# RetNet scores and an MLP on one core: scalings of q and k, their transposes and the loads put into other slots of a tile

## The chip, the core and the metric

The kernel runs on one core of a Trainium2 chip. Time is device microseconds (us) of one execution. The engines are TensorE (PE in the profile; PEld is its weight load), VectorE (DVE), ScalarE (ACT), GpSimd (POOL) and SyncE (SP). Each takes its instructions in its own order and waits on semaphores for the others. DMA transfers are issued from SyncE's queue (outputs and transposes) and GpSimd's (loads), and run on 16 DMA engines.

## What is computed

```python
scores = (1 / sqrt(64)) * q @ k^T                  # q, k, v: 8 batches x 8 heads x 576 x 64
ret = scores * Dmat                                # gamma_h ** (i - j) for i >= j, else 0
x = (ret @ v) as 4608 rows x 512
h = x @ w_in                                       # 512 x 2048
out = (h * tanh(softplus(h))) @ w_out              # 2048 x 512
```

## The kernel before

**Chunks and tiles.** The rows are cut into 36 chunks of 128. Four chunks are a tile; tiles 0 to 8 go through the MLP one after the other. Chunks 0 to 7 are handled in a way of their own. A later chunk n goes through these steps:

- the loads of q and k into `qkraw` and of v into `vs` (`load_part`, L326), issued from GpSimd; `qkraw` has 5 buffers, `vs` 10. A load can be paced (`paced`, L312): it is issued only after a given activation of ScalarE.
- the scaling P(n) (`step_p`, L344): two VectorE instructions at L352 multiply q and k by powers of gamma, row by row, into `qks` (bf16, 6 buffers).
- the transpose T(n) (`step_t`, L355): from chunk 16 on a DMA transpose at L374 on SyncE's queue, from `qks` to `qkT` (6 buffers).
- the scores (`step_s`, L377, products at L386) and the mask (`step_m`, L390, VectorE at L392) for a pair of chunks.
- the states (`states`, L422; products at L432 take `qks` and `vs`, VectorE sums them up at L454 and L456).
- the outputs (`outputs`, `outputs_end`, products at L488 and L504), copied by ScalarE (L516, L561) into `xT`, which the MLP reads.

A *visit* does the outputs of a pair n, n + 1 and the states and scores of the pair after it. `outputs_end` comes in two groups, and the second must not start before the first has been written: `written` (L415) puts a no-op on SyncE's queue that waits for the first group, and TensorE's second group at L504 waits for this no-op. It is called the *marker* here (L417). In a whole visit (`visit`, L518) both groups stand in one slot, with the scores of the next pair between them. In a split one (`visit_first`, L538; `visit_second`, L550) the marker comes four slots ahead of the second group.

**The steady loop** (L1151 to L1243) runs tiles t = 2 to 7. Each has 16 slots i: tile t's first MLP product with its activation (`g1`, L581; ScalarE L587), the second product of tile t - 1 (`unit`, L742, in Strassen's manner with 7 products of half sizes; `g_sum` on VectorE at L650 forms the sums that it takes), and the attention of the next tile. `PLAN` (L1128) lists the jobs of the slots from tile 3 on: g is a `g1`, U a unit, S a `g_sum`, X the sums of `xT`, A and B the two parts of a pair of Strassen blocks in the first product. A (`pair_begin`, L817) makes four products, ScalarE copies two of them (L830, L831), and GpSimd adds them up (L832, L833). B (`pair_end`, L836) makes three more, and VectorE subtracts (L844) and adds (L846); ScalarE's activation L845 then frees the PSUM bank. By slots, A0 is in 2, B0 in 3, A1 in 11, B1 in 12.

With n the first chunk of the half (n = 4(t + 1), + 2 from slot 8 on), a half of a tile from 3 on goes like this, with slots counted from the half's start: P(n + 4) at the end of slot 4, P(n + 5) at the end of slot 5, T(n + 4) and T(n + 5) at the start of slot 7. A whole visit is in slot 6 of its half; split ones are in 2 and 6. Whole are those with n = 16, 20, 22, 26, 28 and 32: the first halves of tiles 3, 4, 6 and 7, the second halves of 4 and 5. In tile 2, P(16) and P(17) are in slots 3 and 5, P(18) and P(19) in 10 and 12; T(16) is in slot 4, T(17) in 7, T(18) in 12, T(19) in 13.

In tiles from 3 on `LOADS` (L1148) places twelve loads: the v's of chunks n + 6 and n + 7 (n of the first half) in slots 2 and 3, their q's and k's in 4 to 7, the v's of n + 8 and n + 9 in 8 and 9, their q's and k's in 11 to 14.

The output rows of tile t - 1 are sent from SyncE (`send`, L610) after unit 9 (VectorE L699, slot 10) and after unit 13 (VectorE L712, slot 15).

Of the kernel before, what the change touches and what calls it, by code (L numbers as in the profile page):

```python
# [9 lines left out]
F32 = mybir.dt.float32  # L10
BF16 = mybir.dt.bfloat16
# [5 lines left out]
def kernel(  # L17
# [19 lines left out]
    B, H, S, D = q.shape  # L37
    assert (B, H, S, D) == (8, 8, 576, 64)
    P = 128
# [5 lines left out]
    NCH = 4  # L45
    NPE = 16
# [17 lines left out]
    io = ctx.enter_context(tc.tile_pool(name="io", bufs=PF))  # L64
    tok = ctx.enter_context(tc.tile_pool(name="tok", bufs=6))
# [12 lines left out]
    live = {}  # L78
# [233 lines left out]
    def paced(ins):  # L312

        while pace:
            behind(ins, pace.pop())
        return ins
# [8 lines left out]

    def load_part(n, part):  # L326
        b, c = chunks[n]
        if n not in live:
            qkr = io.tile([P, 2, H, D], F32, name="qkraw")
            live[n] = {"qkr": qkr, "vs": tok.tile([P, H, D], BF16, name="vs", bufs=10)}  # L330
        qkr, vr = live[n]["qkr"], live[n]["vs"]
        for t, src in (((qkr[:, 0], q), (qkr[:, 1], k), (vr, v))[part],):
            live[n]["landing"] = []
            if c < 4:
                ins = nc.gpsimd.dma_start(out=t, in_=src[b, :, ds(P * c, P), :].rearrange("h p d -> p h d"))  # L335
                live[n]["landing"].append(paced(ins))
            else:
                for e in range(2):
                    ins = nc.gpsimd.dma_start(
                        out=t[ds(64 * e, 64)],  # L340
                        in_=src[b + e, :, ds(512, 64), :].rearrange("h p d -> p h d"))
                    live[n]["landing"].append(paced(ins))
# [131 lines left out]
    def run(jobs, *how):  # L474
        while jobs:
            jobs.pop()(*how)
# [145 lines left out]
    NS = 2  # L622
# [47 lines left out]
    def rest():  # L670
        while behind_visit:
            behind_visit.pop(0)()
# [96 lines left out]
    def w_in_sum_first(i):  # L769

        a, b, op_ = W7[i]
        to = {1: kept[:, 0], 5: kept[:, 1], 6: kept[:, 2]}.get(i)
        if to is None:
            to = w_in_quarter(*{2: (1, 0), 7: (0, 1)}[i])
        nc.vector.tensor_tensor(to, w_in_quarter(*a), w_in_quarter(*b), op=op_)
        w7[i, 0] = to
# [16 lines left out]
    def x_sums(t):  # L793

        if not x_room:
            x_room.append(first.tile([P, 2, H, D], BF16, name="k0", bufs=2).rearrange("p x h d -> p (x h d)"))
            x_room.append(first.tile([P, 2, NP, 64], F32, name="s0", bufs=4)
                          .rearrange("p x n d -> p (x n d)").bitcast(BF16))
            x_room.append(consts.tile([P, hK * hT], BF16, name="xsum"))
        x = lambda j, k: xts[t][:, ds(hK * j, hK), ds(hT * k, hT)]  # L800
        for m, (i, a, b, op_) in enumerate(((3, (0, 1), (1, 1), OP.subtract), (4, (1, 0), (0, 0), OP.subtract),
                                            (6, (0, 0), (0, 1), OP.add), (1, (0, 0), (1, 1), OP.add),
                                            (7, (1, 0), (1, 1), OP.add))):
            x7[i] = x_room[m // 2][:, ts(m % 2, hK * hT)].rearrange("p (c k) -> p c k", c=hK)
            nc.vector.tensor_tensor(x7[i], x(*a), x(*b), op=op_)
        x7[5], x7[2] = x(1, 1), x(0, 0)
# [152 lines left out]
    def att(n, steps):  # L959
        if n >= n_chunks:  # L960
            return
        for step in steps:
            {"P": step_p, "T": step_t}[step](n)
# [117 lines left out]
    for u in range(2, 24):  # L1081
        j, w = divmod(u, 4)
# [54 lines left out]
            pace.append(done[t])  # L1137

    def load_ahead(t, i, so_far):
        for at in (x for x in range(12) if LOADS[x] == i):  # L1140
            m, part = ((0, 2), (1, 2), (0, 0), (0, 1), (1, 0), (1, 1))[at % 6]
            n = NCH * (t + 1) + at // 6 * 2 + 6 + m
            if n < n_chunks:
                if so_far:
                    pace.append(so_far)
                load_part(n, part)

    LOADS = (2, 3, 4, 5, 6, 7, 8, 9, 11, 12, 13, 14)  # L1148
    W_IN = {4: (1, 2), 5: (6, 5), 13: (7,)}
    W_IN_FIRST = {7: 1, 8: 5, 9: 6, 10: 2, 11: 7}  # L1150
    for t in range(NS, nT - 1):  # L1151
        for i in range(nF):
            n, w = NCH * (t + 1) + i // 8 * 2, i % 8
            copies_first = i == 8 and n - 2 in WHOLE
            if w == (2 if t == NS else 0) and not copies_first:
                run(casts, act)
            if t == NS and i in W_IN_FIRST:
                w_in_sum_first(W_IN_FIRST[i])
            if t == nT - 2 and i == 15:
                rest()  # L1160
                x_sums(nT - 1)
            for m in W_IN.get(i, ()) if t == nT - 2 else ():
                w_in_sum(m)
            if (t, i) in HALVED:
                halved[0] = HALVED[t, i]
            for job in PLAN[i] if t > NS else {5: ("S5",), 9: ("S7",)}.get(i, ()):
                if job[0] == "S":
                    g_sum(t - 1, int(job[1]))
                elif job == "X":
                    x_sums(t)  # L1170
            if t == NS:
                if w == 6:
                    visit(n, ((ps_h, "hp"), (ps_h, "hp")), (act, act))
            elif n in WHOLE:
                if w == 6:
                    visit(n, ((ps_h, "hp"), (ps_h, "hp")), (act, act))
                elif w == 7:
                    run(sums)
            elif w == 2 and n < n_chunks:
                visit_first(n)  # L1180
            elif w == 6 and n < n_chunks:
                visit_second(n, act)
            if w == (3 if t > NS else 7 if n + 2 == NPE else 0) or w == 0 and n + 2 == NPE:
                run(sums)
            if w in (0, 1) and n + 2 < NPE:
                att(n + 2 + w, "P")
            if w == 1 and n + 4 == NPE:
                more_loads(n + 7)
            ahead = (2, 4) if n + 2 == NPE else (3, 5)
            if t == NS and w in ahead and n + 4 >= NPE:  # L1190
                att(n + 4 + ahead.index(w), "P")
            if t == NS and i == 11:
                behind_visit.pop(0)()
            if t == NS and i == 13:
                rest()
            if w == 0 and n + 2 == NPE:
                tick(t)
            if w == 7 and n + 4 == NPE:
                att(n + 5, "T")
            if w == (4 if n <= NPE - 2 else 7) and n + 4 >= NPE:  # L1200
                att(n + 4, "T")
            if t == NS and n + 2 >= NPE and w in PACED:
                m, part = ((0, 2), (1, 2), (0, 0), (0, 1), (1, 0), (1, 1))[PACED.index(w)]
                tick(t)
                load_part(n + 6 + m, part)
            if w == 5 and n + 4 < NPE:
                more_loads(n + w + 2)
            if w in (4, 5) and n + 2 < NPE:
                att(n - 2 + w, "T")
            if w == (5 if n + 2 == NPE else 7) and n + 2 >= NPE:  # L1210
                att(n + 5, "T")

            if t == NS:
                if i == 14:
                    for s in (2, 3):
                        send(t - 1, s)
                if w == 6:
                    unit(t - 1, BESIDE[i])
                g1(t, i)
                if i in BESIDE and w != 6:  # L1220
                    unit(t - 1, BESIDE[i])
            else:
                if i == 15:
                    rest()
                so_far = done.get(t)
                jobs = PLAN[i]
                for job in reversed(jobs) if n in WHOLE and w == 6 else jobs:
                    if job[0] == "A":
                        pair_begin(int(job[1]))
                    elif job[0] == "B":  # L1230
                        pair_end(t, int(job[1]))
                    elif job[0] == "g":
                        g1(t, int(job[1:]))
                    elif job[0] == "U":
                        unit(t - 1, int(job[1:]))
                        run(crossed)
                        if copies_first:
                            run(casts, act)
                if w in (4, 5):
                    att(n + w, "P")  # L1240
                load_ahead(t, i, so_far)
                if i == 8:
                    rest()  # L1243
# [32 lines left out]
```

## Time and profile before

| what | value |
|---|---|
| median of 3 runs | 284.32 us (284.06, 284.32, 287.03) |
| profiled execution | 283.5 us |
| its span | 281.8 us |
| mean granted TensorE clock | 0.999 |
| DMA: loads from GpSimd (q0) | 25.44 MB, 66.0% of 16 engines' span |
| DMA: outputs and transposes from SyncE (q1) | 14.69 MB, 28.8% |

A row of a timeline has the start in us from the span's start, the duration, the engine and the line, output and inputs, and how many instructions of one kind were merged; a bracket tells how long the engine had been idle before it, and what ended that. A row of waits has the sum, the times and the longest. SPq is SyncE's sequencer: the duration of a DMA there is the time for which it holds SyncE, not that of the transfer. A row of a stretch of time has each engine's busy time, then the granted clock, the DMA share and GB/s. Tile 3 begins at about 98.8 us, tile 4 at 127.2, tile 5 at 155.6, tile 6 at 184.0 and tile 7 at 212.5; a slot is about 1.8 us.

### The profile page before, as it was taken

How to read it: one execution, taken by the hardware profiler on the slowest of the kernel's cores; microseconds unless marked ns; L12 is line 12 of the kernel's file. 1: busy time of each engine (PE TensorE's matmuls, PEld its weight loads, DVE VectorE, ACT ScalarE, POOL GpSimd, SP SyncE). 2: the span in 40 equal slices, each digit the busy share in tenths (PEclk: the TensorE clock that was granted, in tenths of full speed). 3: DMA queues.
4: the chain of work that ended last, by engine and by line, in shares of the span. 5: the costliest groups of instructions: out<-in, count | busy, mean ns of one | idle time of the engine just before them, and what ended most of it. 6: DMA issues, size and time to landing. Idle time of an engine off the chain costs nothing.

```text
span 281.8 us, 9378 instructions
## 1 busy us (share of the span) xinstructions
PE 275.0 (98%) x4036; PEld 206.0 (73%) x4036; DVE 225.1 (80%) x350; ACT 165.9 (59%) x303; POOL 142.1 (50%) x177
## 2 busy tenths in 40 slices
PE   7899999999999999999999999999999999999994
PEld 3566788988866677667777776777767766888783
DVE  4864679979988978887897978787898786778783
ACT  5555566645886566665675565656566656567620
POOL 8848395877582725472558074718121002559400
PEclk9999999999999999999999999999999999999999
DMA  7999999999999989989999999999956002200333
GB/s 153 158 202 189 193 213 174 192 199 240 185 206 128 178 254 149 148 198 81 231 163 183 119 189 149 238 74 219 105 142 141 2 2 78 74 2 0 113 97 91
DMA packets 77161, 41.24 MB, mean 146 GB/s; under 512 B 60736, under 2 KB 69184, under 8 KB 77120
## 3 DMA queue, kind: packets, MB, share of 16 engines
q0 software_dynamic: 49872, 25.44, 66.0%
q1 hardware_dynamic: 26656, 14.69, 28.8%
q8 instruction: 31, 0.51, 0.8%
q10 hardware_dynamic: 592, 0.52, 0.6%
q14 instruction: 10, 0.08, 0.1%
HBM read 36.70 MB, written 9.44 MB: 164 GB/s over the span
## 4 chain that ended last, share of the span: by engine, by line
PE 93%; DVE 2%; DMA 2%; ACT 1%; issue 1%; POOLq 0%; SPq 0%; POOL 0%; ACTq 0%; DVEq 0%
PE ops L659 28%; PE hp L571 26%; PE hp L598 5%; PE hp L810 5%; PE st L659 5%; PE hp L659 4%; PE hp L576 2%; PE st L810 2%; PE sc L432 2%; DMA gT<-in_q_dram 2%; PE sc L386 2%; PE sc L810 1%; PE sc L923 1%; PE sc L366 1%; PE hp L488 1%; PE hp L504 1%
## 5 line engine op out<-in xcount | busy, mean ns | idle before, releaser
L571 PE MATMUL hp<-xT,w_in_t 128*128 128x512 bf16 x340 | 84.9, 379 | 0.1
L659 PEld LDWEIGHTS <-room 128*128 128x128 bf16 x656 | 63.3, 98 | 15.4
L587 ACT ACTIVATE gT<-hp 128x512 bf16<-128x512 f32 x93 | 55.1, 598 | 30.3 <-PE hp L571 30.2
L650 DVE TENSOR_TENSOR room<-gT 128x2048 bf16<-128x2048 bf16 x43 | 52.5, 1240 | 1.1 <-ACT gT L587 1.1
L571 PEld LDWEIGHTS <-w_in_t 128*128 128x128 bf16 x344 | 33.2, 98 | 27.2 <-issue 0.5
L832 POOL TENSOR_TENSOR k<-k 128x256 f32<-128x256 f32 x10 | 9.5, 951 | 62.2 <-ACT k L830 62.2
L659 PE MATMUL ops<-room,room 128*128 128x256 bf16 x320 | 39.9, 273 | 0.0
L352 DVE TENSOR_TENSOR qks<-qkraw,gqk 128x512 bf16<-128x512 f32 x56 | 35.1, 682 | 0.1
L659 PEld LDWEIGHTS <-gT 128*128 128x128 bf16 x288 | 27.6, 98 | 6.4 <-ACT gT L587 0.4
L659 PE MATMUL ops<-w_out_t,room 128*128 128x256 bf16 x224 | 28.7, 273 | 0.0
L335 POOL DMA_DIRECT2D vs<-in_v_dram x24 | 21.6, 902 | 12.7 <-ACT gT L587 12.7
L335 POOL DMA_DIRECT2D qkraw<-in_q_dram x24 | 21.8, 908 | 9.9 <-DMA vs<-in_v_dram 8.6
L335 POOL DMA_DIRECT2D qkraw<-in_k_dram x24 | 21.6, 899 | 9.8 <-ACT gT L587 9.6
L844 DVE TENSOR_TENSOR k<-k,hp 128x512 f32<-128x512 f32 x10 | 6.9, 686 | 17.7 <-PE hp L810 12.8
L392 DVE TENSOR_TENSOR sm<-sc,mask 128x1024 bf16<-128x1024 f32 x14 | 17.0, 1217 | 2.4 <-PE sc L386 2.3
L598 PE MATMUL hp<-xT,w_in_t 128*128 128x128 bf16 (+1 forms) x184 | 15.3, 240 | 0.0
L456 DVE TENSOR_TENSOR total<-sc,total 128x256 f32<-128x256 f32 x32 | 13.5, 422 | 0.8
L598 PEld LDWEIGHTS <-w_in_t 128*128 128x128 bf16 x184 | 13.1, 98 | 1.1 <-DVE xT L255 0.2
L516 ACT CAST xT<-hp 128x512 bf16<-128x512 f32 x18 | 9.7, 589 | 6.4 <-PE hp L504 6.3
L845 ACT ACTIVATE gT<-hp 128x512 bf16<-128x512 f32 x10 | 6.0, 597 | 11.8 <-DVE k L844 11.8
L601 ACT ACTIVATE gT<-hp 128x512 bf16<-128x512 f32 x16 | 9.6, 600 | 5.4 <-PE hp L598 5.4
L659 PE MATMUL ops<-w_out_t,gT 128*128 128x256 bf16 x96 | 12.5, 273 | 0.0
(205 smaller groups left out, 512.0 us busy)
## 6 DMA issues: line engine op xcount, KB each, us to landing
out_dram<-res SPq DMA_DIRECT2D x29, 256.0 KB, 4.6
qkraw<-in_q_dram POOLq DMA_DIRECT2D x24, 256.0 KB, 5.6
qkraw<-in_k_dram POOLq DMA_DIRECT2D x24, 256.0 KB, 5.9
vs<-in_v_dram POOLq DMA_DIRECT2D x24, 128.0 KB, 4.8
w_out_t<-in_moe_w_out_dram POOLq DMA_DIRECT2D x4, 512.0 KB, 12.0
w_in_t<-in_moe_w_in_dram POOLq DMA_DIRECT2D x6, 256.0 KB, 8.2
out_dram<-res SPq DMA_DIRECT2D x9, 128.0 KB, 2.5
qkraw<-in_q_dram POOLq DMA_DIRECT2D x8, 128.0 KB, 5.2
```

The lines of the kernel that those rows point to most:

```text
L335: ins = nc.gpsimd.dma_start(out=t, in_=src[b, :, ds(P * c, P), :].rearrange("h p d -> p h d"))
L352: nc.vector.tensor_tensor(slots[:, :, y], heads[:, :, y], factors[:, :, y].unsqueeze(3).to_broadcast([P, NP, 2, D]), op=OP.mult)
L392: nc.vector.tensor_tensor(sm.rearrange("p e x n i -> p (e x n) i"), live[n]["sc"].rearrange("p e x n i -> p (e x n) i"), mask.unsqueeze(1) ...
L456: nc.vector.tensor_tensor(new[:, k], st[:, j, x], total[b], op=OP.add)
L516: copy(xts[t][:, :, ds(P * s, 2 * P)].rearrange("p h (x j i) -> p j h x i", x=2, j=2)[:, j], both[j])
L571: nc.tensor.matmul(to, lhsT=w, rhs=x, start=first, stop=last)
L587: done[t] = nc.scalar.activation(gts[t][:, f, :], hp, AX.Mish)
L598: nc.tensor.matmul(hp[:, a].rearrange("p (e k) -> p e k", e=2)[:, e], lhsT=w_in_t[:, c, ts(2 * i + a, P)], rhs=x1[j][:, e, c, :], start=(a ...
L601: nc.scalar.activation(gts[1][:, ds(2 * i, 2), ds(2 * P * j, 2 * P)], hp, AX.Mish)
L650: engine.tensor_tensor(to, g_half(t, *a), g_half(t, *b), op=op_)
L659: nc.tensor.matmul(bank[:, half, :], lhsT=g[:, f, ts(half, P)], rhs=w[:, f, :], start=(f == 0 and half == 0 and not add), stop=(f == hF - ...
L810: nc.tensor.matmul(to, lhsT=w7_of(i, b, c), rhs=x7[i][:, c, :], start=(start and c == 0), stop=(c == hK - 1), skip_group_check=True)
```

## The change

From tile 3 on, with slots of the whole tile:

| | before | after |
|---|---|---|
| P(n + 4), P(n + 5), first half | end of 4, end of 5 | start of 3, start of 4 |
| T(n + 4), T(n + 5), first half | start of 7, both | end of 4, end of 5 |
| P(n + 4), P(n + 5), second half | end of 12, end of 13 | start of 9, start of 11 |
| T(n + 4), T(n + 5), second half | start of 15, both | end of 9, end of 11 |

In tile 2, T(16) and T(17) are both in slot 7, T(18) and T(19) both in slot 15. The loads: `qkraw` and `vs` of a chunk are allocated apart, a slot can hold several loads, and q and k are loaded further ahead: those of n + 8 and n + 9 in slots 7 and 8, those of n + 10 and n + 11 (which were loaded in the next tile) in slots 14 and 15; v of n + 6 and n + 7 comes in slot 0, v of n + 8 and n + 9 in slot 13. Tile 3 loads q and k of six chunks (`LOADS_FIRST`).

In the built program the instructions of TensorE and of ScalarE stand in the same order as before. On VectorE the first scaling of a half stands ahead of L844 and the second behind L846 in the first halves; in the second halves both stand ahead of L844, the first right behind a `g_sum` (L650), the second behind the last state sums (L456, L454) of that place, or the next `g_sum` where there are none. On SyncE the transposes of a first half stand ahead of the marker of slot 6; those of a second half stand on both sides of the sends of slot 10. In tile 2, T(18) and T(19) stand behind four sends.

```diff
     def load_part(n, part):
         b, c = chunks[n]
-        if n not in live:
-            qkr = io.tile([P, 2, H, D], F32, name="qkraw")
-            live[n] = {"qkr": qkr, "vs": tok.tile([P, H, D], BF16, name="vs", bufs=10)}
-        qkr, vr = live[n]["qkr"], live[n]["vs"]
-        for t, src in (((qkr[:, 0], q), (qkr[:, 1], k), (vr, v))[part],):
+        of = live.setdefault(n, {})
+        if part == 2:
+            of["vs"] = tok.tile([P, H, D], BF16, name="vs", bufs=10)
+        elif "qkr" not in of:
+            of["qkr"] = io.tile([P, 2, H, D], F32, name="qkraw")
+        for t, src in ((of["vs"], v) if part == 2 else (of["qkr"][:, part], (q, k)[part]),):
...
     def load_ahead(t, i, so_far):
-        for at in (x for x in range(12) if LOADS[x] == i):
-            m, part = ((0, 2), (1, 2), (0, 0), (0, 1), (1, 0), (1, 1))[at % 6]
-            n = NCH * (t + 1) + at // 6 * 2 + 6 + m
+        for m, part in (LOADS_FIRST if t == NS + 1 else LOADS).get(i, ()):
+            n = NCH * (t + 1) + m
...
-    LOADS = (2, 3, 4, 5, 6, 7, 8, 9, 11, 12, 13, 14)
+    LOADS = {0: ((6, 2), (7, 2)), 7: ((8, 0), (8, 1)), 8: ((9, 0), (9, 1)),
+             13: ((8, 2), (9, 2)), 14: ((10, 0), (10, 1)), 15: ((11, 0), (11, 1))}
+    LOADS_FIRST = {**LOADS, 0: (), 2: ((6, 0),), 3: ((6, 1), (7, 0)), 4: ((7, 1),), 5: ((6, 2), (7, 2))}
+    SCALED, TURNED = {3: 4, 4: 5, 9: 4, 11: 5}, {4: 4, 5: 5, 9: 4, 11: 5}
...
-            if w == 7 and n + 4 == NPE:
-                att(n + 5, "T")
-            if w == (4 if n <= NPE - 2 else 7) and n + 4 >= NPE:
-                att(n + 4, "T")
+            if t == NS and w == 7:
+                for m in (4, 5):
+                    att(n + m, "T")
+            if t > NS and i in SCALED:
+                att(n + SCALED[i], "P")
...
-            if w == (5 if n + 2 == NPE else 7) and n + 2 >= NPE:
-                att(n + 5, "T")
...
-                if w in (4, 5):
-                    att(n + w, "P")
+                if i in TURNED:
+                    att(n + TURNED[i], "T")
                 load_ahead(t, i, so_far)
```

## The prediction

> **What bounds the kernel now.** The first page was read first: the span, the busy shares and the chain of work that ended last.
>
> ```profile
> span 281.8 us, 9378 instructions
> ...
> PE 275.0 (98%) x4036; PEld 206.0 (73%) x4036; DVE 225.1 (80%) x350; ACT 165.9 (59%) x303; POOL 142.1 (50%) x177
> ...
> PE 93%; DVE 2%; DMA 2%; ACT 1%; issue 1%; POOLq 0%; SPq 0%; POOL 0%; ACTq 0%; DVEq 0%
> ```
>
> TensorE is the bound: 275.0 of 281.8 us, and 93% of the chain. Next came TensorE's own waits, six groups of which the first and the last are shown, and the busy time of one steady tile.
>
> ```profile
> PE ops L167 <- DVE room L130: 1.3, 1, 1.3
> ...
> PE st L659 <- ACT gT L587: 0.2, 1, 0.2
> ```
> ```profile
> 98.80:127.20 28.40, 28.40 (x430) 20.43 (x429) 23.46 (x37) 17.89 (x34) 13.98 (x16) 1.00 1.02 187
> ```
>
> All six lie before the tiles that the change touches, or last 0.2 us. In tile 3 TensorE is busy for 28.40 of 28.40 us at the full granted clock (1.00). So moved scalings, transposes and loads can remove no wait of TensorE in this execution: the order of TensorE's instructions is the same in both kernels, and the only question is which new waits the change makes.
>
> **First halves: the transpose is put ahead of the marker.** Before, both scalings of a half stand behind L844 and L846, and both transposes behind the visit and its marker (the SyncE no-op for which TensorE's second group at L504 waits). Now the first scaling goes into slot 3, the second into slot 4, and each transpose right behind its scaling; in tiles 3, 4 and 6, whose first half has a whole visit in slot 6, SyncE meets both transposes before the marker.
>
> ```profile
> 89.77 1.28 DVE L352 TENSOR_TENSOR qks<-qkraw,gqk 128x512 bf16<-128x512 f32 x2
> ...
> 106.49 0.69 DVE L844 TENSOR_TENSOR k<-k,hp 128x512 f32<-128x512 f32 x1 [2.85 <-PE hp L810]
> ...
> 107.89 1.28 DVE L352 TENSOR_TENSOR qks<-qkraw,gqk 128x512 bf16<-128x512 f32 x2
> ...
> 136.25 1.28 DVE L352 TENSOR_TENSOR qks<-qkraw,gqk 128x512 bf16<-128x512 f32 x2
> ...
> 193.12 1.28 DVE L352 TENSOR_TENSOR qks<-qkraw,gqk 128x512 bf16<-128x512 f32 x2
> ```
> ```profile
> 91.20 1.24 SPq L374 DMA_TRANSPOSE qkT<-qks  x1
> ...
> 93.68 1.24 SPq L374 DMA_TRANSPOSE qkT<-qks  x1
> ...
> 110.16 1.24 SPq L374 DMA_TRANSPOSE qkT<-qks  x1
> 111.56 3.19 SPq L374 DMA_TRANSPOSE qkT<-qks  x1
> ...
> 138.47 1.25 SPq L374 DMA_TRANSPOSE qkT<-qks  x1
> ...
> 195.28 1.25 SPq L374 DMA_TRANSPOSE qkT<-qks  x1
> ```
> ```profile
> 110.14 0.32 PE L504 MATMUL hp<-qkT,ssb 64*64 64x64 bf16 x16
> ```
>
> The first scaling costs nothing: a pair lasts 1.28 us and VectorE stands idle for 2.85 us before L844. The GpSimd additions of the same pair of blocks lie in that gap as well; two of 0.72 us (below) and the scaling make 2.7 us even one after the other. Without that gap it would cost its 1.2 us on L844.
>
> The second scaling then takes the place of the first: it ends at 107.89 + 1.28 = 109.17. A transpose that waits for its scaling starts 0.15 us after it (89.77 + 1.28 = 91.05, then 91.20), holds SyncE for 1.24, and the next instruction there starts 0.16 later (110.16 + 1.24 = 111.40, then 111.56). So SyncE passes the marker at 109.17 + 0.15 + 1.24 + 0.16 = 110.72. Before, the transpose behind the marker starts at 110.16, and TensorE goes on at 110.14: both leave the marker together. TensorE, with no slack there, loses 0.56 us. Tile 4: 137.53 + 1.55 = 139.08 against 138.47, 0.61. Tile 6: 194.40 + 1.55 = 195.95 against 195.28, 0.67. Sum 1.8 us.
>
> The unknown term is how long a transpose holds SyncE there. One that follows another after 2.5 us held it for 1.24 (93.68), one that follows after 1.4 us for 3.19 (111.56). The new distance is over 4 us, so I take 1.24; the other end would add 1.95 us three times. Below zero it cannot go, since TensorE waits for the same marker in both kernels. In tile 5 the first half has its marker in slot 2, ahead of both transposes: nothing.
>
> The Trainium skill ("DMA: Bandwidth & Descriptors", section "Issuing engines are not separate DMA queues") says that the sequencer's time to start a DMA is usually small beside the DMA itself. By that rule this term is near zero, and the total below becomes 2.8 us. The rows here show 1.24 to 3.19 us of SyncE for one transpose, which is not small beside the margin of the marker, so I do not go by it; it stands behind a rival.
>
> **Second halves: a scaling is put ahead of L844.** Here the scalings go into slots 9 and 11, ahead of L844 in slot 12, where VectorE has less room.
>
> ```profile
> 118.96 1.21 DVE L650 TENSOR_TENSOR room<-gT 128x2048 bf16<-128x2048 bf16 x1
> 120.10 0.42 DVE L456 TENSOR_TENSOR total<-sc,total 128x256 f32<-128x256 f32 x1
> ...
> 121.60 0.69 DVE L844 TENSOR_TENSOR k<-k,hp 128x512 f32<-128x512 f32 x1 [0.62 <-POOL k L833]
> ...
> 146.58 1.22 DVE L650 TENSOR_TENSOR room<-gT 128x2048 bf16<-128x2048 bf16 x1
> 149.21 0.69 DVE L844 TENSOR_TENSOR k<-k,hp 128x512 f32<-128x512 f32 x1 [1.42 <-POOL k L833]
> ...
> 160.87 1.33 DVE L456 TENSOR_TENSOR total<-sc,total 128x256 f32<-128x256 f32 x3
> ...
> 177.78 0.69 DVE L844 TENSOR_TENSOR k<-k,hp 128x512 f32<-128x512 f32 x1 [1.42 <-POOL k L833]
> ...
> 207.11 0.68 DVE L844 TENSOR_TENSOR k<-k,hp 128x512 f32<-128x512 f32 x1
> ```
> ```profile
> 119.53 1.24 POOL L832 TENSOR_TENSOR k<-k 128x256 f32<-128x256 f32 x1 [1.45 <-ACT k L830]
> 120.84 0.72 POOL L833 TENSOR_TENSOR k<-k,one 128x256 f32<-128x256 f32 x1
> ...
> 147.42 0.96 POOL L832 TENSOR_TENSOR k<-k 128x256 f32<-128x256 f32 x1 [0.98 <-ACT k L830]
> ...
> 161.40 0.72 POOL L832 TENSOR_TENSOR k<-k 128x256 f32<-128x256 f32 x1 [7.74 <-ACT k L830]
> ```
> ```profile
> 122.32 0.60 ACT L845 ACTIVATE gT<-hp 128x512 bf16<-128x512 f32 x1 [1.69 <-DVE k L844]
> ...
> 123.36 0.59 ACT L709 COPY dmask<-ops 128x512 f32<-128x512 f32 x1
> ...
> 150.42 0.59 ACT L587 ACTIVATE gT<-hp 128x512 bf16<-128x512 f32 x1
> ...
> 207.82 0.60 ACT L845 ACTIVATE gT<-hp 128x512 bf16<-128x512 f32 x1 [1.88 <-DVE k L844]
> ...
> 208.79 0.59 ACT L709 COPY dmask<-ops 128x512 f32<-128x512 f32 x1
> ```
> ```profile
> 123.70 1.04 PE L571 MATMUL hp<-xT,w_in_t 128*128 128x512 bf16 x4
> ...
> 150.95 0.55 PE L488 MATMUL hp<-sm,vs 64*64 64x64 bf16 x32
> ...
> 209.04 1.04 PE L571 MATMUL hp<-xT,w_in_t 128*128 128x512 bf16 x4
> ```
>
> Behind L844 wait, in ScalarE's order, L845 (which frees a PSUM bank), the activation L587 and the copy L709; TensorE takes their banks 0.1 to 0.8 us after. The scaling of slot 9 falls into the wait for L699's product, and TensorE sets L699 again; that of slot 11 is what delays L844.
>
> A new question is GpSimd. L832 adds two operands in SBUF: 1.24 and 0.96 us beside L650, whose two operands are in SBUF, but 0.72 beside L456, which has one in PSUM. In the first two it ends 0.59 us after L650 does (120.17 and 147.80): it had waited for it. A scaling has two SBUF operands too, so I take it that scaling and additions exclude each other; that VectorE waits in turn is not shown.
>
> The Trainium skill ("SBUF — State Buffer", section "Who interferes with whom") states this: a VectorE instruction with two SBUF inputs and a GpSimd instruction that reads SBUF contend. These rows agree with it as far as GpSimd's side goes; by it the sum is 4.6 us, without it 2.5.
>
> Tile 3: L456 and its neighbour, 0.45 apiece, end at 121.00. Alone the scaling would then run until 122.20 and L844 come 0.60 late, still hidden (L845 would end at 123.52, before 123.70). Held by L833 until 121.56, it ends at 122.76: L844 is 1.16 late, L845 ends at 124.08 instead of 122.92, and TensorE is 0.4 late at 123.70; L709, at 125.11, adds 0.1. So 0.5.
>
> Tile 4: from 147.72 (L650 gives way 1.14 after its start) the scaling alone would end at 148.92, before 149.21: nothing. Turn by turn with the two additions (147.72 + 2 x 0.72 + 1.20 = 150.36) L844 is up to 1.1 late; L832 overlapped L650's end by 0.13 at its turn, and three turns bring that to 0.8. L587 ends at 151.01 and its bank is wanted by the row of 150.95, in its second half, so nearly all shows: 0.8. Tile 5 has the same order and the same wait of 1.42: 0.8.
>
> Tile 6: four L456 end only when L844 starts, and GpSimd is done by then. The scaling's 1.20 goes on L844 in full; L845 ends at 209.62 against 209.04, 0.6, and L709 adds 0.1: 0.7, whatever GpSimd does.
>
> Sum: 0.5 + 0.8 + 0.8 + 0.7 = 2.8 us; bounds 0.7 (no exclusion) and 1.2 x 4 = 4.8.
>
> **Loads and the late transposes.**
>
> ```profile
> qkT<-qks SPq DMA_TRANSPOSE x20, 8.7
> ```
> ```profile
> L335 POOL DMA_DIRECT2D qkraw<-in_q_dram x24 | 21.8, 908 | 9.9 <-DMA vs<-in_v_dram 8.6
> ```
>
> The same loads are issued, most of them earlier; tile 3 issues six chunks in place of four. Six loads now stand on GpSimd between slot 14 and slot 0, 6 x 0.91 = 5.5 us, ahead of L832 in slot 2; its 7.74 us of idle time cover them. If that cover went, L832 would come late to L844. Steady transposes land earlier than before, which TensorE does not notice here. In tile 2 they are later: both of the first half in slot 7 and both of the second in slot 15, behind four output sends. Issued at about 85.2 and 86.5, the first pair is read at about 95.5; with a median of 8.7 us to land the second has 0.3 us to spare. I cost it at nothing, with up to 3 us if it is late.
>
> **Sum.** 1.8 + 2.8 = 4.6 us. The profiled execution took 283.5 us, 281.8 of it span, so it would take 288.1. The median of the runs is 284.3, 0.8 above it; against that, 288.9.
>
> **The rivals.** (1) Scaling and additions do not exclude each other: 1.8 + 0.7 = 2.5, 286.8 us. For it: VectorE is never seen waiting for GpSimd's port. Against it: L832's 0.72 and 1.24. (2) The 1.24 us of a transpose run on behind SyncE and the marker passes at once: the first halves cost nothing and 2.8 stays, 287.1. Against it, the next instruction starts 0.16 after the 1.24 are over (111.56). The Trainium skill's page on DMA, named above, speaks for this one. (3) A late pair in tile 2, or a SyncE hold nearer 3.19: 4.6 + 1.5 to 3 = 290.4 to 292; it decides when the second transpose lands over 9 us after its issue. (4) Not slower: the timed runs exceed the profiled one because transposes land late in them, which earlier transposes cure, and both new waits find slack in TensorE. Its price is at most 284.3 - 283.5 = 0.8, so 283.5; it decides only if the marker is not what TensorE waits for at 110.14. The two leaving together speaks against it.
>
> **How the numbers follow.** About 1% is what a measurement of this kernel can tell from no change; that is 281.5 and 287.2 us. The forecast has 0.50 (own range 287.4 to 290.2), rival (1) 0.22, (2) 0.08, (3) 0.12, (4) 0.08. Slower by over 1%: nearly all of the forecast, (3) and half of (2), 0.64. Faster: 0.02, from (4), for what the trace does not show. The rest, 0.34, is within 1%. The range leaves out (4), and the ends of (1) and (3): 286.0 to 291.0.
>
> **What would show it.** In the profile after: TensorE idle of 0.5 to 0.7 us before L504 in slot 6 of tiles 3, 4 and 6, put down to the marker; L844 of the second halves coming 0.8 to 1.2 us later behind the slot-11 scaling, with that scaling or an addition drawn out; TensorE idle behind L845, L587 or L709. A transpose that holds SyncE for 3 us, or TensorE waiting at L386 for a transpose, would make it wrong upward; no idle time at L504, downward.

## The result, and the profile after

| | before | after |
|---|---|---|
| median | 284.19 us (6 runs) | 288.50 us (6 runs, 288.38 to 288.98) |
| ratio to before, with its 95% interval | | 1.0142 [1.01, 1.0185] |
| profiled execution; its span | 283.5; 281.8 us | 288.43; 286.7 us |

Slower by 1.4%; the forecast was 288.9 us in a range of 286 to 291. Runs over 1.5% above the fastest run of their kernel are left out of every ratio here; the one profile of the loads alone is of such a run (292.67 us), and nothing here rests on it.

In the changed kernel most lines have numbers higher by one: L352 is L353, L374 L375, L417 L418, L504 L505, L844 and L846 are L845 and L847, L832 and L833 are L833 and L834, L845 is L846, L587 L588. The page of the changed kernel, as the first fence of the prediction had it for before:

```profile
span 286.7 us, 9337 instructions
...
PE 275.1 (96%) x4008; PEld 206.7 (72%) x4036; DVE 227.0 (79%) x350; ACT 165.7 (58%) x303; POOL 147.9 (52%) x177
...
PE 78%; DVE 8%; issue 4%; DMA 3%; POOL 3%; ACT 2%; POOLq 0%; SPq 0%; ACTq 0%; DVEq 0%
```

TensorE's work is the same (275.1 us against 275.0), the span is 4.9 us longer, and VectorE, GpSimd and ScalarE have got into the chain of work. GpSimd's busy time rose by 5.8 us with the same 177 instructions; a part of that is waiting that the records count as work, as will be seen. TensorE's own waits, largest first:

```profile
PE hp L489 <- ACT gT L846: 1.3, 2, 1.1
...
PE hp L572 <- ACT gT L846: 0.8, 2, 0.6
PE hp L505 <- SPq L418: 0.6, 3, 0.2
PE hp L489 <- ACT gT L588: 0.5, 2, 0.3
```

None of these four stood in the list of before. Three waits at L505 are for the marker; the others are for activations behind the subtraction L845. Since TensorE's 4036 weight loads are recorded in full in every trace and stand in the same order, the starts of the same loads can be compared: the table gives how many us a kernel is behind the trace of before when that trace is at the time in the head. The column of 95 us is the start-up, which differs from run to run; a loss is the difference between two columns.

| kernel | 95 | 112 | 126 | 141 | 154 | 181 | 197 | 281 |
|---|---|---|---|---|---|---|---|---|
| changed | -0.09 | 0.45 | 0.83 | 1.27 | 2.92 | 3.68 | 4.18 | 4.90 |
| slot-11 scaling behind | 0.32 | 0.87 | 0.87 | 1.30 | 3.17 | 5.06 | 5.56 | 5.53 |
| transpose behind marker (2nd profile) | 0.04 | 0.06 | 0.48 | 0.48 | 2.48 | 3.24 | 3.24 | 3.97 |
| both | 0.62 | 0.64 | 0.64 | 0.64 | 2.89 | 4.98 | 4.98 | 4.95 |
| no GpSimd sums | -0.17 | 0.74 | 0.74 | 1.18 | 1.34 | 1.23 | 1.73 | 2.46 |
| both, transposes behind both visits | 0.06 | 0.08 | 0.08 | 0.09 | 0.88 | 0.88 | 0.88 | 0.86 |
| second halves as before | 1.13 | 1.16 | 1.16 | 1.16 | 1.18 | 1.19 | 1.19 | 1.15 |
| loads and tile 2 only | 0.98 | 1.01 | 1.01 | 1.01 | 1.04 | 1.04 | 1.04 | 1.01 |

In the changed kernel the markers of tiles 3, 4 and 6 (columns 112, 141, 197) took 0.54 + 0.44 + 0.50 = 1.5 us, the second halves of tiles 3, 4, 5 and 6 (126, 154, 181, 281) 0.38 + 1.65 + 0.76 + 0.72 = 3.5.

A marker, in tile 4 (VectorE, SyncE and TensorE of the changed kernel):

```profile
137.08 1.28 DVE L353 TENSOR_TENSOR qks<-qkraw,gqk 128x512 bf16<-128x512 f32 x2
```
```profile
138.43 1.24 SPq L375 DMA_TRANSPOSE qkT<-qks  x1
```
```profile
139.77 0.26 PE L505 MATMUL hp<-qkT,ssb 64*64 64x64 bf16 x8 [0.17 <-SPq L418]
```

The scaling ends at 138.36, the transpose starts 0.07 later and holds SyncE for 1.24, until 139.67; TensorE goes on 0.10 after that, released by the marker.

A second half, in tile 4 (VectorE, GpSimd, ScalarE, TensorE):

```profile
148.27 1.21 DVE L651 TENSOR_TENSOR room<-gT 128x2048 bf16<-128x2048 bf16 x1
149.40 1.28 DVE L353 TENSOR_TENSOR qks<-qkraw,gqk 128x512 bf16<-128x512 f32 x2
152.10 0.69 DVE L845 TENSOR_TENSOR k<-k,hp 128x512 f32<-128x512 f32 x1 [1.42 <-POOL k L834]
```
```profile
148.69 2.58 POOL L833 TENSOR_TENSOR k<-k 128x256 f32<-128x256 f32 x1 [1.26 <-ACT k L831]
151.34 0.72 POOL L834 TENSOR_TENSOR k<-k,one 128x256 f32<-128x256 f32 x1
```
```profile
152.82 0.60 ACT L846 ACTIVATE gT<-hp 128x512 bf16<-128x512 f32 x1 [3.31 <-DVE k L845]
```
```profile
153.47 0.22 PE L489 MATMUL hp<-sm,vs 64*64 64x64 bf16 x2 [1.08 <-ACT gT L846]
```

GpSimd's addition L833, 0.72 us of work, begins at 148.69 and ends at 151.27: 0.6 us after the scaling ends (150.68). It has waited through L651 and through both instructions of the scaling. Then L834, L845 and L846 follow, and TensorE stands for 1.08 us. In tile 5 the same two meet the other way round:

```profile
179.20 2.35 DVE L353 TENSOR_TENSOR qks<-qkraw,gqk 128x512 bf16<-128x512 f32 x2
```
```profile
178.63 1.24 POOL L833 TENSOR_TENSOR k<-k 128x256 f32<-128x256 f32 x1 [2.76 <-ACT k L831]
179.94 1.06 POOL L834 TENSOR_TENSOR k<-k,one 128x256 f32<-128x256 f32 x1
```

Here GpSimd goes ahead, and the scaling takes 2.35 us in place of 1.28.

### The profile page after: what moved, and what is told of

Same layout as the page of the kernel before. It is cut to its first block, busy times and chain, and to the rows that moved or that the text cites. A ratio compares the mean times of both kernels' runs of the same rounds, so it can differ in the third digit from the quotient of the medians.

```text
span 286.7 us, 9337 instructions
## 1 busy us (share of the span) xinstructions
PE 275.1 (96%) x4008; PEld 206.7 (72%) x4036; DVE 227.0 (79%) x350; ACT 165.7 (58%) x303; POOL 147.9 (52%) x177
## 4 chain that ended last, share of the span: by engine, by line
PE 78%; DVE 8%; issue 4%; DMA 3%; POOL 3%; ACT 2%; POOLq 0%; SPq 0%; ACTq 0%; DVEq 0%
PE ops L660 24%; PE hp L572 22%; PE hp L599 5%; PE st L660 5%; PE hp L660 4%; PE hp L811 4%; DMA w_in_t<-in_moe_w_in_dram 3%; DVE qks L353 3%; DVE room L651 2%; PE hp L577 2%; PE sc L811 1%; PE st L811 1%; PE sc L433 1%; PE sc L924 1%; POOL gT L111 1%
## 5 line engine op out<-in xcount | busy, mean ns | idle before, releaser
L572 PE MATMUL hp<-xT,w_in_t 128*128 128x512 bf16 x314 | 82.2, 379 | 2.4 <-ACT gT L846 0.8
L588 ACT ACTIVATE gT<-hp 128x512 bf16<-128x512 f32 x93 | 55.1, 598 | 30.1 <-PE hp L572 27.4
L651 DVE TENSOR_TENSOR room<-gT 128x2048 bf16<-128x2048 bf16 x43 | 52.5, 1241 | 1.1 <-ACT gT L588 1.1
L833 POOL TENSOR_TENSOR k<-k 128x256 f32<-128x256 f32 x10 | 14.2, 1420 | 57.4 <-ACT k L831 57.4
L353 DVE TENSOR_TENSOR qks<-qkraw,gqk 128x512 bf16<-128x512 f32 x56 | 37.9, 720 | 0.8 <-DMA qkraw<-in_k_dram 0.8
L846 ACT ACTIVATE gT<-hp 128x512 bf16<-128x512 f32 x10 | 6.0, 597 | 16.4 <-DVE k L845 16.4
L845 DVE TENSOR_TENSOR k<-k,hp 128x512 f32<-128x512 f32 x10 | 6.8, 683 | 10.9 <-PE hp L811 8.0
```

What stands on the lines that cost most here:

```text
L353: nc.vector.tensor_tensor(slots[:, :, y], heads[:, :, y], factors[:, :, y].unsqueeze(3).to_broadcast([P, NP, 2, D]), op=OP.mult)
L572: nc.tensor.matmul(to, lhsT=w, rhs=x, start=first, stop=last)
L588: done[t] = nc.scalar.activation(gts[t][:, f, :], hp, AX.Mish)
L651: engine.tensor_tensor(to, g_half(t, *a), g_half(t, *b), op=op_)
L833: nc.gpsimd.tensor_tensor(z[:, 0], z[:, 0], z[:, 1], op=OP.add)
```

## The experiments

The theory: of the 4.9 us, a transpose ahead of the marker makes 1.5, and the scaling of slot 11, with the GpSimd additions that it excludes and that exclude it, the rest. The diffs are against the changed kernel unless another is named.

**The scaling of slot 11 behind the Strassen part.**

```diff
-    SCALED, TURNED = {3: 4, 4: 5, 9: 4, 11: 5}, {4: 4, 5: 5, 9: 4, 11: 5}
+    SCALED, TURNED = {3: 4, 4: 5, 9: 4}, {4: 4, 5: 5, 9: 4, 12: 5}
...
+                if i == 12:
+                    att(n + 5, "P")
```

> Changed kernel, with only the scaling of slot 11 put behind the second Strassen part of slot 12 (its transpose behind it); everything else stays moved. My theory: the 3.3 us that TensorE loses in the second halves of tiles 3 to 6 come from this scaling standing ahead of the subtraction L845; they vanish and the 1.2 to 1.3 us at the markers of the first halves stay: about 285.2 us, ratio to before 1.004. Rival A (the loads, now further ahead, or the transposes that land earlier make the loss): no change, 288.5. Rival B (the slot-9 scaling does it too): about half stays, 286.8.

Measured: 288.84 us, ratio 1.0151 [1.0119, 1.0183]. Read by its time alone, rival A would stand. The trace says otherwise: the losses of tiles 3 and 6 are gone (0.87 to 0.87, 5.56 to 5.53). In tile 4 the addition L833 begins when it did in the changed kernel (148.72, 148.69) and is short (GpSimd, VectorE):

```profile
148.72 1.34 POOL L833 TENSOR_TENSOR k<-k 128x256 f32<-128x256 f32 x1 [1.25 <-ACT k L831]
```
```profile
150.90 0.69 DVE L845 TENSOR_TENSOR k<-k,hp 128x512 f32<-128x512 f32 x1 [1.42 <-POOL k L834]
```

It takes 1.34 us in place of 2.58, and L845 begins 1.2 us earlier. VectorE stands idle for 1.42 us before L845, in which the scaling's 1.28 would have found room; so what cost the 1.2 us in the changed kernel is the addition that waited, not VectorE's own time.

But a new loss stands in tiles 4 and 5, whose second halves have a whole visit in slot 14, with a marker of its own. SyncE and TensorE in tile 4:

```profile
153.65 1.27 SPq L375 DMA_TRANSPOSE qkT<-qks  x1
```
```profile
155.03 0.32 PE L505 MATMUL hp<-qkT,ssb 64*64 64x64 bf16 x16 [1.27 <-SPq L418]
```

My edit put the transpose of slot 12 ahead of that marker, and it waits there for its scaling. That costs 1.47 us in tile 4 and 1.88 in tile 5, a little more than the 3.1 that the edit had saved. Tile 4 loses 1.87 in all; the other 0.40 stands ahead of the marker, and the scaling of slot 9 is what is left for it. The edit was badly chosen, and it shows the first mechanism at three to four times its size.

**The second transpose of the first halves behind the visit.**

```diff
-    SCALED, TURNED = {3: 4, 4: 5, 9: 4, 11: 5}, {4: 4, 5: 5, 9: 4, 11: 5}
+    SCALED, TURNED = {3: 4, 4: 5, 9: 4, 11: 5}, {4: 4, 6: 5, 9: 4, 11: 5}
```

> Changed kernel, with only the second transpose of each first half put behind the visit of slot 6 (at the end of the slot, not at the end of slot 5); its scaling stays in slot 4. My theory: this transpose held SyncE ahead of the marker; the 0.4 us before L505 in tiles 3, 4 and 6 vanish, 1.2 to 1.3 in all: about 287.2 us, ratio 1.010. Rival (the marker is late for another reason, for example because its own wait ends late): no change, 288.5.

Measured: 288.49 us, 287.07 to 290.62 in 4 runs, ratio 1.0121 [1.0079, 1.0163]: by time undecided. A second run of the same kernel:

> The kernel with only the second transpose of each first half put behind the visit, a second time: its first profile has no wait at the three markers, as my theory says, but a granted clock of 0.66 from 155 to 160 us and 1.5 us more in the start-up, so that its time does not show the 1.3 us. My theory: about 287.2 us by the undisturbed runs (clock 0.999 or more), against 288.5 of the changed kernel, and no step before L505 in slot 6. Rival (removing the marker's wait makes a new loss of the same size): 288.5 at the full clock, with new waits in the trace between 99 and 213 us.

Measured: 287.61 us, ratio 1.0135 [1.0097, 1.0174]; four of six runs gave 287.42 to 287.69, two 289.65. That is 0.4 us above the theory and 0.9 below the rival. The list of TensorE's waits has no row of L505 any more, and the table shows nothing at the three markers (0.04 to 0.06, 0.48 to 0.48, 3.24 to 3.24). So the markers' 1.5 us come from that transpose. Of these, 1.1 reach the end (3.97 - 0.04 in place of 4.90 + 0.09), since tile 4's second half now takes 2.00 in place of 1.65: in the changed kernel the waits for the markers had hidden 0.4 us of another loss, as the section on the prediction works out.

**Both edits.** The two diffs above together.

> Both edits together: slot-11 scaling behind the second Strassen part, second transpose of the first halves behind the visit. The earlier loads, the first scalings in slots 3 and 9, the second of the first halves in slot 4 and the transposes of tile 2 stay moved. My theory: the two losses are all there is (4.6 of 4.9 us) and add up: about 284.0, ratio 1.00; if late transposes were what made the runs of before scatter upward, 283.6 with a spread under 0.5. Rival (the losses only change place, since the scaling behind the second Strassen part delays the later work of VectorE): 285.5 to 287.

Measured: 288.20 us, ratio 1.0123 [1.0091, 1.0155], above the theory and the rival. The table has the places: nothing at 112, 126, 141, 197 and 281, but 2.25 us in tile 4 and 2.09 in tile 5. The list of waits:

```profile
PE hp L505 <- SPq L418: 3.2, 2, 1.9
```

Two waits for the marker of slot 14 hold the loss that the first experiment made; it hid the sum of the two edits. The other 0.8 of tile 4 stand ahead of the marker.

**Both edits, with each second transpose behind its visit.**

```diff
-    SCALED, TURNED = {3: 4, 4: 5, 9: 4, 11: 5}, {4: 4, 5: 5, 9: 4, 11: 5}
+    SCALED, TURNED = {3: 4, 4: 5, 9: 4}, {4: 4, 6: 5, 9: 4, 14: 5}
...
+                if i == 12:
+                    att(n + 5, "P")
```

> The kernel with both edits, and the second transpose of the second halves put behind the visit of slot 14 as well, at its end (in the run with both edits it stood in slot 12, ahead of the marker of the whole visits in tiles 4 and 5, and TensorE waited there 1.45 and 2.09 us). My theory (a transpose that waits for its scaling ahead of a marker holds SyncE, and TensorE pays): these 3.5 us vanish, 0.75 in tile 4 stays, for which the scaling of slot 9 is named: 284.7 us, 1.0 above the profiled run of before at most. Rival (the work only moves on: something else becomes late once more, such as the transpose itself at its reader): 286 or more, with TensorE waiting for a transpose at L387.

Measured: 284.62 us, ratio 1.0011 [0.9992, 1.003]. The wait for the marker is gone, and of 4.9 us 0.8 is left, all of it in tile 4. This is what the theory forecast. Its rows there (VectorE, GpSimd):

```profile
145.63 1.29 DVE L353 TENSOR_TENSOR qks<-qkraw,gqk 128x512 bf16<-128x512 f32 x2
146.83 0.68 DVE L700 TENSOR_TENSOR res<-ops,res 128x512 f32<-128x512 f32 x1
147.43 1.22 DVE L651 TENSOR_TENSOR room<-gT 128x2048 bf16<-128x2048 bf16 x1
150.06 0.69 DVE L845 TENSOR_TENSOR k<-k,hp 128x512 f32<-128x512 f32 x1 [1.42 <-POOL k L834]
```
```profile
147.50 1.72 POOL L833 TENSOR_TENSOR k<-k 128x256 f32<-128x256 f32 x1 [1.25 <-ACT k L831]
```

The scaling of slot 9 puts the sum L651 off from 146.58 (before) to 147.43. GpSimd's addition begins at the same time as before (147.50, 147.42), but now has nearly all of L651 ahead of it and takes 1.72 us in place of 0.96.

**Second halves as before.** The first halves as in the experiment above, the second halves with the slots of before.

```diff
-    SCALED, TURNED = {3: 4, 4: 5, 9: 4, 11: 5}, {4: 4, 5: 5, 9: 4, 11: 5}
+    SCALED, TURNED = {3: 4, 4: 5}, {4: 4, 6: 5}
...
+            if t > NS and i == 15:
+                for m in (4, 5):
+                    att(n + m, "T")
...
+                if i in (12, 13):
+                    att(n + i - 8, "P")
```

> First halves as in the changed kernel, but with the second transpose behind the visit of slot 6; scalings and transposes of the second halves of tiles 3 to 7 in the slots that they had before; the earlier loads and tile 2 stay changed. My theory: the scaling of slot 9 costs the 0.75 us in tile 4 by itself, since it delays the sum L651 behind it and so the GpSimd addition L833 that waits for L651: here these vanish too, TensorE loses nothing in tiles 3 to 7, about 284.0 us, 0.75 below the kernel with only the slot-11 scaling moved back. Rival (the 0.75 comes from the loads, which GpSimd issues at other times): 284.7, L489 of tile 4 still late. If late transposes are what scatters the runs of before, the spread here is under half of theirs.

Measured: 283.77 us (283.20 to 284.62 in 12 runs), ratio 0.998 [0.9964, 0.9996]. TensorE loses 0.02 us after 95 us, and the addition in tile 4 is short again:

```profile
148.58 0.95 POOL L833 TENSOR_TENSOR k<-k 128x256 f32<-128x256 f32 x1 [1.26 <-ACT k L831]
```

So the 0.8 of tile 4 belonged to the scaling of slot 9. This kernel is a fifth of a per cent faster than the kernel before, by an interval that just leaves out 1; TensorE had no wait there to lose, and the last experiments look for the reason.

**Without the GpSimd additions.** This kernel leaves L833 and L834 out; the cross sums of the Strassen blocks are missing.

```diff
-        nc.gpsimd.tensor_tensor(z[:, 0], z[:, 0], z[:, 1], op=OP.add)
-        nc.gpsimd.tensor_tensor(z[:, 1], z[:, 0], one, op=OP.add)
```

> Changed kernel without the two GpSimd additions L833 and L834; the cross sums of the Strassen blocks are then missing from the result, VectorE subtracts from what ScalarE copied. My theory (the VectorE scaling and the GpSimd additions hold each other up at the port they share): the losses of the second halves of tiles 3, 4 and 5 (0.28 + 1.62 + 0.76 = 2.7 us) vanish nearly whole, the 0.65 of tile 6, where GpSimd is done before the scaling begins, and the 1.2 at the markers stay: about 286.0, ratio 1.006. Rival (it is only the 1.2 us of VectorE's own time ahead of the subtraction): the stalls in tiles 3 to 6 stay at 0.6 to 1 each, 288 or more.

Measured: 286.04 us, ratio 1.006 [1.0038, 1.0082], near the theory's 286.0. The second halves of tiles 3, 4 and 5 lose 0.00, 0.16 and less than nothing; tile 6 keeps its 0.7 and the markers of tiles 4 and 6 their 0.44 and 0.50. The 0.91 of column 112 is a wait for a transpose, which covers the one for the marker of tile 3 and which none of the other profiles in the table has:

```profile
PE sc L387 <- DMA qkT<-qks: 0.8, 1, 0.8
```

It is the second transpose of slot 15 of tile 2, issued at 100.73 and landed 9.9 us later; in the changed kernel the same one took 6.0 us and was in time. VectorE in tile 4:

```profile
149.31 1.29 DVE L353 TENSOR_TENSOR qks<-qkraw,gqk 128x512 bf16<-128x512 f32 x2
150.51 0.68 DVE L843 TENSOR_TENSOR k<-k,hp 128x512 f32<-128x512 f32 x1
```

The scaling's own 1.2 us ahead of the subtraction does no harm there: the subtraction (L843 in this kernel) begins at 150.51 where it began at 152.10, and the two traces differ by 0.1 us until there. This kernel also takes away the subtraction's wait for the additions, so by itself it shows only that the scaling's own time is not the cause. With the rows of tiles 4 and 5 and the short addition of the first experiment, what does the harm in tiles 3 to 5 is the addition that waits for the scaling, or makes it wait.

**The loads alone.** The kernel before with the changed `load_part`, `load_ahead` and `LOADS` of the diff, and nothing else.

> The kernel before with only the new places of the loads (and q, k and v of a chunk allocated apart); all scalings and transposes where they were before. My theory: the loads cost TensorE nothing, 284.3 us, ratio 1.00. Rival A (a part of the 4.9 us comes from the loads, by GpSimd's issue time ahead of its additions): 285 to 286. Rival B (the loads further ahead are a gain that the scalings hide): under 283.5.

Measured: 284.69 us, ratio 0.999 [0.9966, 1.0015]; single runs reached 292.67. No cost of the loads can be told from this, and in the trace with the loads and tile 2 changed (last row of the table) TensorE loses 0.03 us after 95 us.

**Which edit makes the runs even.** The two kernels above with the changed tile 2 and at most 0.8 us lost had their runs close together (284.23 to 285.42 and 283.20 to 284.62). Three kernels divide this up: the changed kernel with the scalings and transposes of tiles 3 to 7 as before (loads and tile 2 are left), the one with second halves as before with the old loads, and the kernel before with only the transposes of tile 2 moved.

```diff
-    SCALED, TURNED = {3: 4, 4: 5, 9: 4, 11: 5}, {4: 4, 5: 5, 9: 4, 11: 5}
...
-            if t > NS and i in SCALED:
-                att(n + SCALED[i], "P")
+            if t > NS and w == 7:
+                for m in (4, 5):
+                    att(n + m, "T")
...
-                if i in TURNED:
-                    att(n + TURNED[i], "T")
+                if w in (4, 5):
+                    att(n + w, "P")
```

> The changed kernel with all scalings and transposes of tiles 3 to 7 in their slots of before; what stays changed are the loads and the two pairs of transposes in tile 2 (slots 7 and 15). In the run with the loads alone the times reached from 283.3 to 292.67, and its profile shows TensorE waiting 1.3 us at L387 for a transpose of tile 2. Theory 1 (the earlier transposes of tiles 3 to 7 bring the runs together): the median is 284.3 to 284.7 and single runs above 286 remain, as before. Theory 2 (the places in tile 2 do it): all runs between 283.2 and 285, as with the second halves as before.

> The kernel with second halves as before and the second transpose of the first halves behind the visit (283.77 us in its run), but with all loads in the places of the kernel before. Theory 1 (scalings and transposes alone make the narrow spread, the loads add nothing): 283.8 us, all runs below 285.5. Rival (the loads further ahead are what the narrow spread comes from): median 284.3 and single runs above 286, as before.

The third, against the kernel before:

```diff
-            if w == 7 and n + 4 == NPE:
-                att(n + 5, "T")
-            if w == (4 if n <= NPE - 2 else 7) and n + 4 >= NPE:
-                att(n + 4, "T")
+            if t == NS and w == 7:
+                for m in (4, 5):
+                    att(n + m, "T")
+            if t > NS and w == 7:
+                for m in (4, 5):
+                    att(n + m, "T")
...
-            if w == (5 if n + 2 == NPE else 7) and n + 2 >= NPE:
-                att(n + 5, "T")
```

> The kernel before with only the transposes of tile 2 moved (both of the first half to slot 7, both of the second to slot 15, behind the sends); loads, scalings and all other transposes as before. Theory (these places alone bring the runs together): median 283.8, no run above 286.1, against single runs of 287 to 293.8 of the kernel before. Rival (it takes the loads or the transposes of tiles 3 to 7 as well): runs above 287 remain, median 284.3.

| kernel | median | range of 12 runs | ratio |
|---|---|---|---|
| loads and tile 2 | 283.78 | 283.44 to 284.56 | 0.9976 [0.9957, 0.9996] |
| second halves and loads as before | 283.78 | 283.43 to 286.04 | 0.9968 [0.9934, 1.0002] |
| tile 2 alone | 283.91 | 283.40 to 285.03 | 0.9965 [0.9931, 1.0] |

The five kernels with tile 2 changed and at most 0.8 us lost (60 runs) never took more than 286.04 us; of the 86 runs of the kernel before beside the experiments, 15 took more than 286.5, and with the loads alone 3 of 13. So in kernels without the new waits the places in tile 2 go with even runs and a median 0.6 to 0.7 us lower, alone or not; two of the three intervals reach 1, and with the old loads one run, of 286.04, went over the 285.5 that its theory allowed. Kernels with the changed tile 2 that lose more can scatter all the same: 287.07 to 290.62 with the transpose behind the marker, 287.08 to 289.22 with both edits. Why the places matter stays open: in the trace of before TensorE waits for no transpose.

## Why the prediction was right, and where it was not

- **No gain is in it for TensorE's waits.** Right: tiles 3 to 7 had none to remove, and no trace here ends earlier than that of before.
- **First halves, 1.8 us.** The mechanism was right (moving one transpose behind the marker makes the three waits vanish), the term 0.3 too large. The transpose holds SyncE for 1.24, as taken. The steps beside it were shorter: 0.07 from scaling to transpose where 0.15 was used, and 0.10 from the transpose's end to TensorE, where the 0.16 of a transpose behind a transpose was put in. By the Trainium skill's rule ("DMA: Bandwidth & Descriptors", "Issuing engines are not separate DMA queues") this term would have been near zero; the transpose behind the marker settles it for the rows. Rival (2) fell.
- **Second halves, 2.8 us; measured 3.5.** Tiles 3, 5 and 6 were 0.5, 0.8 and 0.7, and measured 0.4, 0.8 and 0.7. Tile 4 was mis-sized: 0.8 against 1.65.
- **The step that failed in tile 4** is in both of its terms. The first is the sentence that the scaling of slot 9 falls into the wait for L699's product. In the trace of before VectorE is idle ahead of L699 for 1.07, 1.28 and 1.15 us in tiles 3, 5 and 6, but in tile 4 only for this:

```profile
145.97 0.69 DVE L699 TENSOR_TENSOR res<-ops,res 128x512 f32<-128x512 f32 x1 [0.32 <-issue]
```

The scaling takes 1.2, and what does not fit goes on through L651 and GpSimd's addition to L845. That costs 0.8 us in the kernel with the transposes behind both visits. In the changed kernel it costs 0.4, by the first experiment: there TensorE, which had lost time at the markers, was 1.27 us behind the trace of before ahead of this place, but VectorE's first L651 only 0.90 (145.33 against 144.43), so that a part of the delay was hidden. The second term is the scaling of slot 11: 0.8 were taken, by turns of VectorE and GpSimd, and 1.2 are measured, its whole length (1.65 - 0.40 in the changed kernel; 2.00 - 0.79 where no marker is late). GpSimd got no turn until VectorE's row of instructions was over.
- **Exclusion** was the choice against rival (1), and the runs bear it out: the addition of tile 4 takes 1.34 us in place of 2.58 with the scaling elsewhere, and without the additions the three tiles lose 0.05 us in all. That VectorE waits in turn, which the prediction called not shown, stands in the rows of tile 5. The Trainium skill ("SBUF — State Buffer", "Who interferes with whom") has it that a VectorE instruction with two SBUF inputs contends with a GpSimd instruction that reads SBUF, and the trace agrees: 2.58 us and 2.35 us for 0.72 and 1.28.
- **Loads and late transposes, nothing.** Right in the changed kernel, and rival (3) did not come there: the median time of a transpose to land fell, from 8.7 us to this:

```profile
qkT<-qks SPq DMA_TRANSPOSE x20, 4.5
```

The prediction priced the first pair of tile 2 alone. The pair of slot 15 is the one that was late once, by 0.8 us in the kernel without the GpSimd additions.
- **The base.** The prediction added its sum to the median of before (284.3) and not to the profiled time (283.5). The profiled time would have been the better base: 288.5 less the 5.0 us between the columns 95 and 281 is 283.5. Rival (4) fell as a case, since both waits reached TensorE, but its price of 0.8 was in the right place: tile 2 gives 0.6 to 0.7. Its cure was not, for the transposes of tile 2 are issued later, not earlier. A base 0.8 too high and a sum 0.4 too low (4.6 against 5.0) leave the forecast 0.4 above. That it came so close is in part luck: these two cancel in part, and so do the 0.3 too much in the first halves and the 0.85 too little in tile 4.

## What to carry to other kernels

Before work is moved into an engine's idle slot, ask what stands behind that slot in its queue and how much idle time there is in that very place: 0.32 us of it do not hide 1.2. A DMA that waits for its data ahead of a semaphore marker in the same queue becomes a wait of whoever waits for the marker, so markers go first. And an experiment that moves work must be read by its trace: here an edit removed its loss and made another of about its size further on, so that its time alone spoke for the wrong theory.

## What was not expected of the hardware

VectorE instructions with two SBUF operands that follow each other without a gap kept GpSimd's addition out for all three of them, 2.58 us (2.94 in the second profile of the transpose behind the marker). In tile 5, with the same row of instructions, GpSimd got in after the first. What decides between the two stays open.

The granted clock can halve behind a wait of TensorE. In the first profile of the transpose behind the marker TensorE stood idle for 1.40 us until 154.52, and from 156.0 on the clock was at 0.50 for about 3 us; the stretches show the length, TensorE, its weight load, VectorE, ScalarE and GpSimd, then the clock:

```profile
155.00:156.00 1.00, 0.99 (x110) 0.99 (x109) 0.05 (x1) 0.96 (x2) 1.00 (x2) 0.99 1.65 145
156.00:157.00 1.00, 1.00 (x23) 0.68 (x11) 1.00 (x1) 0.71 (x2) 1.00 (x2) 0.50 1.48 94
157.00:158.00 1.00, 1.00 (x6) 0.68 (x5) 0.97 (x4) 0.36 (x1) 0.14 (x1) 0.50 1.70 246
158.00:159.00 1.00, 0.78 (x2) 0.29 (x2) 0.97 (x3) 0.00 (x0) 0.00 (x0) 0.50 1.05 254
```

In this profile tile 4 took 1.6 us more than in the second one of the same kernel (3.63 against 2.00 between the columns 141 and 154), where the same wait of 1.4 us left the clock at 1.00. A wait of 1.94 us with both edits, until 185.29, left it there too, so what lowers it stays open. The Trainium skill ("TensorE: Matmul & The Clock Gate", "Part 1: The HAM clock gate") puts the idle window that lowers the clock at some 3.4 us; the wait here was shorter.
